# Six DMA transposes of an attention-then-experts kernel moved to TensorE, and their matmuls to earlier slots

## The chip, the cores and the metric

The kernel runs on one core of one Trainium2 chip. The metric is the device time of one execution in microseconds (us).

## The reference, cut to what matters

The first half is attention without softmax: scores are scaled by a decay that depends on the head and on the distance between positions, and masked to be causal. The second half passes every token through four experts and adds their outputs with normalised weights.

```python
# q, k, v: [8 batches, 8 heads, 576 positions, 64]
scores = scale * np.matmul(q, k.transpose(0, 1, 3, 2))
ret = scores * Dmat[None, :, :, :]          # gamma[h] ** (i - j) where i >= j, else 0
attn_out = np.matmul(ret, v)
x = attn_out.transpose(0, 2, 1, 3).reshape(4608, 512)
p = domain_probs / (domain_probs.sum(-1, keepdims=True) + 1e-09)
for e in range(4):                          # w1[e]: 512 x 1024, w2[e]: 1024 x 512
    h = np.maximum(x @ w1[e], 0.0)
    out += p[:, e:e + 1] * (h @ w2[e])
```

## The kernel before

The 4608 tokens are cut into nine tiles of 512. A batch has 576 positions, so tile 0 is batch 0 without its last 64 positions (its "remainder"). Tile 1 needs that remainder and most of batch 1. While TensorE does the expert matmuls of a tile, the attention of the next one is slipped in between them. The expert work of tile 0 is numbered in 32 slots: for each of the four experts four "up" groups (x @ w1, eight 128x512 matmuls, 1.73 us) and four "down" pieces (h @ w2, eight more). After each slot the work registered for it is run:

```python
    for e in range(E):
        for i in range(4):
            up_group(h, 0, e, i)
            run(slots, n)
            n += 1
        for m in range(4):
            down_plain(h, 0, e, m)
            run(slots, n)
            n += 1
```

Batch 1 comes in four "units": unit 0 and 1 are its first 256 positions, for the first and the last four heads, units 2 and 3 the next 256. A unit is cast to bf16 with its decays, k and q are transposed, then follow the scores, the state (`kv`) and the values. In the kernel before, batch 0's units, in the prologue, are transposed on TensorE (`trans_pe`); the remainder and batch 1's units are transposed by DMA from SBUF (the on-chip memory) to SBUF, issued on SyncE's queue:

```python
        # class Unit
        def trans_pe(self, between=0):
            self.qk = atp.tile([128, 2, 2, 2, C], BF16, tag="qkT", name="qkT0")
            pt = ring_tile("pt", [128, 2, 2, 2, 2 * C], BF16)
            for i, n in ((1, "k"), (0, "q")):
                # ... cut
                for r in range(2):
                    for g in range(2):
                        nc.tensor.transpose(pt[:, i, r, g, 0:C], self.bf(n)[:, r, 2 * g:2 * g + 2]..., ident)
            nc.scalar.activation(self.qk..., pt..., Copy)

        def trans_dma(self):
            self.qk = atp.tile([128, 2, 2, 2, C], BF16, tag="qkT", name="qkT1")
            for i, n in ((1, "k"), (0, "q")):
                nc.sync.dma_start_transpose(out=self.qk[:, i]..., in_=self.bf(n)...)
```

The tag `qkT` has two buffers: unit 2 cannot be transposed before unit 0's values have read theirs. The slots, before:

```python
    remainder(slots, 0, (-1, 13, 24, 25))        # cast and transposes, scores, values

    def v_cast(u):
        vs[u].cast("k", nc.vector)
        vs[u].cast("q", nc.vector)
        vs[u].cast("v", nc.scalar)
        vs[u].trans_dma()
        if u == 0:
            load_v(3)

    for u, (c, sc, o) in enumerate(((17, 26, 27), (18, 27, 28), (24, 28, 29), (25, 29, 30))):
        add(c, lambda u=u: v_cast(u))
        add(o, lambda u=u: vs[u].values())
        add(sc, lambda u=u: v_head(u))           # scores and state
    add(26, lambda: [load_p(1, e, nc.sync) for e in range(E)])
    add(27, lambda: load_pair(raw1, 2, 0))       # tile 1's own loads, SyncE's queue too
    add(27, lambda: load_rem(1))
```

Meanwhile the weights (fp32 in HBM, cast to bf16 by the DMA) and batch 1's inputs come in on GpSimd's queue:

```python
    load_w2(2)
    load_v(0)
    load_v(1)
    load_w1(3)
    load_v(2)
    load_w2(3)
```

## Time and profile before

| | before |
|---|---|
| median of 3 runs | 549.27 us (548.95 to 550.24) |
| span of the profiled run | 547.2 us, mean granted TensorE clock 0.997 (1 is full speed) |
| TensorE busy | 529.8 us (97%) |
| tile 0, first up matmul to tile 1's first | 20.11 to 91.33 us: 71.22 us |
| tile 1, the same | 91.33 to 149.81 us: 58.48 us |

The two lines of TensorE's timeline (start, length, what) that bound tile 0:

```profile
20.11 3.12 PE L345 MATMUL ph<-xt,w 128*128 128x512 bf16 x12
91.33 10.52 PE L345 MATMUL ph<-xt,w 128*128 128x512 bf16 x47
```

The page shows the span in 40 slices, each digit a share in tenths (9 is 90% or more):

```profile
PE   8999959999999999999999999999999999999997
PEclk9999989999999999999999999999999999999999
DMA  9999956966446552755177526662555311010001
```

The one dip of TensorE and of its clock between the start and the end is in the sixth slice, 68 to 82 us. The view of waits of TensorE from 48 to 92 us (who waited for whom: us in total, times, longest) names it:

```profile
PE s L526 <- DMA qkT<-bf_q: 5.2, 1, 5.2
PE s L526 <- DMA qkT<-q: 1.1, 1, 1.1
PE ph L345 <- issue: 0.2, 1, 0.2
PE o L589 <- DVE sbd L561: 0.2, 1, 0.2
PE po L364 <- issue: 0.2, 1, 0.2
```

The busy times by stretch, from the end of slot 15 to tile 1:

```profile
core 0: us, PE busy (x) PEld busy (x) DVE busy (x) ACT busy (x) POOL busy (x), PEclk, DMA share, GB/s
48.05:67.60 19.55, 19.45 (x99) 8.78 (x99) 13.79 (x21) 7.98 (x10) 5.40 (x7) 1.00 1.15 226
67.60:72.78 5.18, 0.01 (x3) 0.04 (x2) 1.39 (x2) 0.06 (x1) 0.00 (x0) 1.00 1.26 189
72.78:77.10 4.32, 4.10 (x47) 2.19 (x52) 1.52 (x2) 2.24 (x4) 0.00 (x0) 0.61 0.00 0
77.10:91.33 14.23, 12.46 (x201) 7.10 (x204) 10.06 (x15) 4.90 (x19) 0.00 (x0) 1.00 0.62 153
```

TensorE does nothing for 5.17 us, then works at a granted clock of 0.61 in the mean of 4.32 us (the trace has 0.50 from 72.78 to 76.19 us, then 1.00). The DMA engines are full (1.15 and 1.26: the share is the time of the packets over that of 16 engines, so here packets overlap) until exactly the moment when the gap ends, and then fall idle (0.00). The chain of work that ended last (start, length, what) passes through the same transpose:

```profile
40.15 11.95 DMA rx<-in_q_dram
52.11 20.53 DMA qkT<-bf_q
72.64 0.14 issue
72.78 0.64 PE s L526 x14
73.42 0.85 PE kvp L545 x16
74.27 0.54 PE ph L345
...
78.94 3.03 DMA qkT<-q
81.98 0.14 issue
82.11 0.44 PE s L526 x16
```

Unit 0's q was given to the queue at 52.11 us and landed 20.5 us later; unit 2's, in an emptier queue, took 3.0 us.

### The profile page before, as it was taken

To read this page: it belongs to the slowest core of one execution; us is meant where nothing else is said; L and a number is where in the kernel's file an instruction comes from. 1 tells how busy PE (TensorE), PEld (TensorE's weight loads), DVE (VectorE), ACT (ScalarE), POOL (GpSimd) and SP (SyncE) were. 2 spreads that over 40 slices of the span, in tenths; PEclk is the share of its full clock that TensorE was granted. 3 is DMA by queue.
4 is the path that set the end of the run, shared out by engine and by line. 5 is a ranking of instruction groups with operands and counts; after the bars stand their busy time and mean duration, and the time that the engine had idled before them with its cause. 6 is when DMAs were issued, how large, how long until landed. Compare 5 with 4: busy or idle time off the path is not lost.

```text
span 547.2 us, 10257 instructions
## 1 busy us (share of the span) xinstructions
PE 529.8 (97%) x4255; PEld 340.5 (62%) x4295; DVE 364.6 (67%) x484; ACT 109.2 (20%) x251; POOL 93.1 (17%) x126
## 2 busy tenths in 40 slices
PE   8999959999999999999999999999999999999997
PEld 4544435458844885478646874588448844884486
DVE  5425638986578666886588648865786667557764
ACT  4623331112202230222112211132012200000010
POOL 5734000211112121111112031112021100000000
PEclk9999989999999999999999999999999999999999
DMA  9999956966446552755177526662555311010001
GB/s 240 202 211 248 215 77 174 209 129 139 113 89 142 125 131 67 158 123 146 55 136 170 139 63 115 140 155 78 110 133 107 83 59 38 24 56 19 1 26 52
DMA packets 148126, 64.27 MB, mean 117 GB/s; under 512 B 127248, under 2 KB 138896, under 8 KB 148080
## 3 DMA queue, kind: packets, MB, share of 16 engines
q1 hardware_dynamic: 137760, 44.22, 36.4%
q0 software_dynamic: 10176, 19.27, 16.2%
q8 instruction: 33, 0.54, 0.4%
q10 hardware_dynamic: 144, 0.13, 0.1%
q14 instruction: 13, 0.11, 0.1%
HBM read 53.56 MB, written 9.51 MB: 115 GB/s over the span
## 4 chain that ended last, share of the span: by engine, by line
PE 81%; DMA 11%; DVE 2%; SPq 1%; POOL 1%; issue 1%; ACT 0%; DVEq 0%
PE ph L345 40%; PE pd L437 36%; DMA qkT<-bf_q 4%; DMA wx<-in_moe_w_dram 3%; DMA rx<-in_q_dram 2%; SPq L119 1%; DVE h L351 1%; PE kvp L261 1%; PE s L274 1%; DMA raw_3v<-in_v_dram 1%; PE o L291 1%; DMA qkT<-q 1%; PE o L284 1%; PE po L364 0%; DVE sbd L561 0%
## 5 line engine op out<-in xcount | busy, mean ns | idle before, releaser
L345 PE MATMUL ph<-xt,w 128*128 128x512 bf16 x1118 | 253.2, 380 | 3.2 <-DVE h L351 1.2
L345 PEld LDWEIGHTS <-w 128*128 128x128 bf16 x1152 | 111.3, 98 | 130.8 <-issue 3.0
L351 DVE SCALAR_TENSOR_TENSOR h<-ph,pB 128x1024 bf16<-128x1024 f32 x128 | 155.8, 1222 | 51.0 <-PE ph L345 50.5
L437 PEld LDWEIGHTS <-h 128*128 128x128 bf16 x1024 | 99.2, 98 | 14.1
L437 PEld LDWEIGHTS <-s 128*128 128x128 bf16 x768 | 74.7, 98 | 9.1
L437 PE MATMUL pd<-wx,h 128*128 128x256 bf16 x512 | 61.2, 273 | 0.0
L437 PE MATMUL pd<-wx,s 128*128 128x256 bf16 x512 | 61.2, 273 | 0.0
L222 POOL DMA_DIRECT2D pB<-pd x28 | 15.9, 568 | 165.4 <-DVE h L351 133.7
L266 ACT ACTIVATE sbd<-kvp 64x256 bf16<-64x256 f32 x48 | 18.2, 378 | 104.6 <-PE kvp L261 104.3
L472 POOL TENSOR_TENSOR ob<-v,p 128x256 f32<-128x256 f32 x15 | 10.9, 726 | 153.7 <-DVE v L469 92.7
L276 DVE TENSOR_TENSOR sT<-s,tri 128x1024 bf16<-128x1024 f32 x24 | 29.2, 1217 | 2.2 <-PE s L274 2.2
L454 DVE TENSOR_TENSOR u<-pd,p 128x256 f32<-128x256 f32 x16 | 6.8, 425 | 35.7 <-PE pd L437 35.7
L437 PE MATMUL pd<-t2w,s 128*128 128x256 bf16 x256 | 30.6, 273 | 0.0
L437 PE MATMUL pd<-t3w,h 128*128 128x256 bf16 x256 | 30.6, 273 | 0.0
L437 PE MATMUL pd<-t4w,h 128*128 128x256 bf16 x256 | 30.6, 273 | 0.0
L245 POOL TENSOR_TENSOR bf_q<-raw_q,gq 128x512 bf16<-128x512 f32 x24 | 25.6, 1069 | 22.7 <-DMA raw_q<-in_q_dram 22.4
L364 PE MATMUL po<-wx,h 128*128 128x512 bf16 x124 | 28.4, 379 | 0.4 <-issue 0.2
L445 ACT ACTIVATE p<-pd 128x256 f32<-128x256 f32 x16 | 6.1, 384 | 94.8 <-PE pd L437 83.8
L309 POOL TENSOR_TENSOR bfr_q<-rawr_q,gqr 64x512 bf16<-64x512 f32 x7 | 11.7, 1669 | 71.6 <-DMA out_dram<-acc 42.2
L456 DVE TENSOR_TENSOR oa<-pd,u 128x256 f32<-128x256 f32 x16 | 6.8, 425 | 23.7 <-PE pd L437 23.7
L349 ACT ACTIVATE h<-ph 128x1024 bf16<-128x1024 f32 x16 | 16.4, 1022 | 30.4 <-PE ph L345 29.1
L418 DVE TENSOR_TENSOR s<-h,s 128x1024 bf16<-128x1024 bf16 x32 | 22.4, 739 | 0.0
(141 smaller groups left out, 393.8 us busy)
## 6 DMA issues: line engine op xcount, KB each, us to landing
pB<-pd POOLq DMA_DIRECT2D x28, 256.0 KB, 3.9
raw_k<-in_k_dram SPq DMA_DIRECT2D x48, 128.0 KB, 2.7
raw_q<-in_q_dram SPq DMA_DIRECT2D x48, 128.0 KB, 3.0
raw_v<-in_v_dram SPq DMA_DIRECT2D x48, 128.0 KB, 3.7
wx<-in_moe_w_dram POOLq DMA_DIRECT2D x4, 1024.0 KB, 17.3
out_dram<-oa SPq DMA_DIRECT2D x16, 256.0 KB, 2.1
out_dram<-ob SPq DMA_DIRECT2D x15, 256.0 KB, 2.0
w<-in_moe_w_dram POOLq DMA_DIRECT2D x3, 1024.0 KB, 15.6
```

The costliest lines, as they stand in the source:

```text
L222: eng.dma_start(out=pB[t, e], in_=pd[e:e + 1, t * NT:(t + 1) * NT].to_broadcast([128, NT]))
L245: nc.gpsimd.tensor_tensor(self.bf["q"], raw["q"], gq[:, :, 2 * p:2 * p + 2].unsqueeze(3).to_broadcast([128, NC, 2, D]), op=MULT)
L266: nc.scalar.activation(sbd[r, self.p, :, r], kvp[r, :, :], Copy)
L276: nc.vector.tensor_tensor(self.sT[:, :, :, :].rearrange("p j c t -> p (j c) t"), s[:, :, :, :].rearrange("p j c t -> p (j c) t"), tri[:, : ...
L309: q_engine.tensor_tensor(bfr["q"][0:R], rawr["q"][0:R], gqr[0:R].rearrange("p (g j) -> p g j", j=2).unsqueeze(3).to_broadcast([R, NP, 2, D ...
L345: nc.tensor.matmul(ph[:, f, :], lhsT=w1_sb[e][:, dc, fc * 128:(fc + 1) * 128], rhs=x[:, dc, :], start=(dc == 0), stop=(dc == NDC - 1))
L349: nc.scalar.activation(h[:, fk:fk + 2, :], ph, Relu)
L351: nc.vector.scalar_tensor_tensor(h[:, fk:fk + 2, :], ph, 0.0, pB[t, e][:, :].unsqueeze(1).to_broadcast([128, 2, NT]), op0=MAX, op1=MULT)
L364: nc.tensor.matmul(po[:, g, :], lhsT=h[:, e * NFC + fc, ns * 128:(ns + 1) * 128], rhs=wx[e // 2][:, (e % 2) * NFC + fc, :, :].rearrange("p ...
L418: nc.vector.tensor_tensor(self.alloc("s4")[:, l], h[:, r, self.a], self.s2[:, l], op=SUB)
L437: mm = nc.tensor.matmul(dst, lhsT=src[:, kk, tok], rhs=rhs(c), start=(start and c == 0), stop=(c == KH - 1), skip_group_check=True)
L472: nc.gpsimd.tensor_tensor(self.ob[:, HF:Dm], self.v, self.p5, op=ADD)
```

## The change

The intent: take the six transposes that compete with the loads (remainder k and q, unit 0 and 1 k and q) off the DMA queue, and spread the matmuls that depend on them over the slots of the third and fourth expert. Units 2 and 3 stay on the DMA queue. The diff, with small cuts:

```diff
-    ident = epool.tile([128, 128], BF16)
+    ident = const.tile([128, 128], BF16)
@@ class Rem
-        def trans_dma(self):
+        def alloc_trans(self):
             self.kT = atp.tile([128, NP, 128], BF16, tag="kTr", name="kTr", bufs=1)
             self.qT = atp.tile([128, NP, R], BF16, tag="qTr", name="qTr", bufs=1)
+
+        def trans_pe(self):
+            self.alloc_trans()
+            pt = ring_tile("ptr", [128, 2, NP, 128], BF16)
+            for i, n, w in ((0, "k", 128), (1, "q", R)):
+                for p in range(NP):
+                    nc.tensor.transpose(pt[:, i, p, 0:w], bfr[n][0:w, p, :, :].rearrange("p j d -> p (j d)"),
+                                        ident[0:w, 0:w])
+            nc.scalar.activation(self.kT, pt[:, 0], Copy)
+            nc.scalar.activation(self.qT, pt[:, 1, :, 0:R], Copy)
+
+        def trans_dma(self):
+            self.alloc_trans()
@@ def remainder
-        l, c, s, o = at
+        l, c, tr, s, o = at
-        add(c, x.trans_dma)
+        add(tr, x.trans_pe)
@@ slots
-    remainder(slots, 0, (-1, 13, 24, 25))
+    remainder(slots, 0, (-1, 13, 15, 16, 17))
-        vs[u].trans_dma()
+        if u > 1:
+            vs[u].trans_dma()
-    for u, (c, sc, o) in enumerate(((17, 26, 27), (18, 27, 28), (24, 28, 29), (25, 29, 30))):
+    for u, (c, tr, sc, o) in enumerate(((17, 20, 22, 23), (19, 22, 24, 25), (24, 0, 28, 29), (25, 0, 29, 30))):
+        if u < 2:
+            add(tr, lambda u=u: vs[u].trans_pe())
-    for j, ats in enumerate(((18, 18, 19, 19), (20, 20, 21, 21), (28, 28, 29, 29), (30, 30, 40, 41))):
+    for j, ats in enumerate(((18, 18, 19, 20), (20, 21, 23, 23), (28, 28, 29, 29), (30, 30, 40, 41))):
```

The last pair of lines moves sums of expert weights on VectorE by a slot or two.

## The prediction

> **What bounds the kernel now.** TensorE. The page gives it 97% of a 547.2 us span, and from tile 1 on the chain of waits is almost only its matmuls (57.8 us a tile). The exception is the end of tile 0. Busy times by stretch: from 67.6 to 72.8 us TensorE is idle 5.17 of 5.18 us. The view of waits names one wait, 5.2 us, of batch 1's first score matmuls for a DMA transpose of q, issued at 52.1 us and landed 20.5 us later (the chain; the median is 2.5 us), as it shares the DMA engines with weight and input loads (DMA share 1.15 to 1.26, 190 to 226 GB/s). From 72.8 to 77.1 the granted clock is 0.61: the eight 128x512 matmuls there take 2.8 us, not 1.7, scores and kv 0.5 us more than later. [...] Unit 2's queued transposes cost one more wait of 1.1 us at 81 us; other small waits (state copies) about 0.7 us.
>
> **What the change does.** Six of tile 0's ten DMA transposes (remainder, units 0 and 1) become 24 TensorE transposes plus four ScalarE copies. Work moves from slots 24 to 28 to slots 15 to 25.
>
> - Removed: 5.2 us idle, about 1.6 us of slow clock, 1.1 us wait for unit 2 (its buffer comes free earlier, the queue is empty): 7.9 us, all on the critical path.
> - Added on TensorE: in the prologue four 128x128 transposes show 0.39 to 0.40 us with 0.22 us latency each, so about 60 to 85 ns a piece in a stream: 1.5 to 2.0 us for 24.
> - Added on ScalarE: two copies of 1.02 us, two of about 0.4 to 0.6 us; it was busy 8 of 19.6 us here: off the path.
> - Moved: sums of weights on VectorE, which has 14 of 19.6 us in this stretch; I estimate waits of a few tenths. PSUM has four buffers, one held by the down product: three are left for scores, state, transposes and values. New waits 0.3 to 0.8 us in all.
> - Unit 3's inputs landed at 71 to 72.7 us. Without the transposes they should land earlier; its cast now comes at about 70 us, so VectorE may wait 1 us, with slack before unit 3 is needed at about 79 us.
>
> Net 7.9 − 1.8 − 0.5: about 5.6 us, kept to the end, as tile 1 onward is TensorE-bound with the same work. Tile 1 should begin at about 85.5 us instead of 91.3.
>
> **Predicted: 543.5 us**, 8 in 10 between 541.3 and 546.2. Faster by over 2% (below 538.3) 0.04; within 2% 0.94; slower 0.02. All idle time and slow clock of this stretch, 8.9 us, are 1.6%, so 2% is out of reach unless something else moves.
>
> **What the profile would show.** No TensorE gap over 1 us between 48 and 86 us; granted clock 1.00 throughout; no wait for a DMA transpose of q; 24 more matmuls onto the identity, 60 to 90 ns net each; transposes of units 2 and 3 landing in 2.5 to 4 us; unit 3's inputs landing before 71 us; tile 1's first up matmul at 84.5 to 86.5 us; later tiles unchanged at 57.8 us.
>
> **What would make it wrong.** A new wait in TensorE's order: transposes standing before ready matmuls while the cast or a PSUM buffer is late; VectorE held by unit 3's late inputs, delaying the output accumulation and so a PSUM buffer; the second-half w2 weights late, which the old gap hid; tile 1's own loads (mixing weights, remainder, first pair) late because TensorE now arrives 6 us sooner. Any could give back 1 to 4 us.

## The result, and the profile after

| | before | after |
|---|---|---|
| median | 549.64 us (4 runs, 548.95 to 550.24) | 542.55 us (4 runs, 542.08 to 542.85) |
| ratio, 95% interval | | 0.9871 (0.9854 to 0.9888) |
| span of the profiled run | 547.2 us | 540.9 us |
| tile 0 | 71.22 us | 64.78 us (20.64 to 85.42) |
| tile 1 | 58.48 us | 58.05 us (85.42 to 143.47) |

The lines that bound tile 0 in the kernel after:

```profile
20.64 2.69 PE L358 MATMUL ph<-xt,w 128*128 128x512 bf16 x10
85.42 7.93 PE L358 MATMUL ph<-xt,w 128*128 128x512 bf16 x36
```

A ratio is the mean time of one kernel's fast runs over that of the other's of the same rounds, so not quite the ratio of the medians quoted. The time fell by 7.1 us by the medians and by 6.3 us between the two profiled spans; the runs of before scatter by more than a microsecond, so the sharper measure is the length of tile 0, read from the trace: 6.44 us less. With the 0.43 us of tile 1, and 0.53 us by which the first up matmul came later in this profile, the span is accounted for (−6.44 − 0.43 + 0.53 = −6.34). That start lies between 20.1 and 20.9 us in all profiles, so I take its shift for run-to-run scatter, not for an effect of the change.

The scatter of before goes with the clock. Besides the profiled run, 29 runs of the kernel before have mean granted clock 0.989 to 0.997, 27 of them at 0.995 or below, and the lower the clock, the longer the run (eight at 0.994 took 549.4 us in the mean, nine at 0.991 or below 550.5 us). The profiled run, at 0.997, is at the mild end, so the slow clock probably cost most runs more than the profile shows; no trace of such a run was kept. The four runs of after have 0.999 to 1.000.

The slices of after:

```profile
PE   8999999999999999999999999999999999999997
PEclk9999999999999999999999999999999999999999
DMA  9999947765265635655277517653654211110001
```

Both dips of the sixth slice are gone. TensorE's waits from 48 to 92 us are down to one line:

```profile
PE o L602 <- DVE sbd L574: 0.2, 1, 0.2
```

By stretch:

```profile
core 0: us, PE busy (x) PEld busy (x) DVE busy (x) ACT busy (x) POOL busy (x), PEclk, DMA share, GB/s
48.58:66.20 17.62, 17.62 (x153) 9.00 (x152) 11.65 (x19) 9.23 (x14) 5.39 (x7) 1.00 1.08 253
66.20:72.00 5.80, 5.80 (x71) 2.84 (x69) 5.60 (x10) 4.40 (x9) 0.00 (x0) 1.00 0.04 12
72.00:77.00 5.00, 5.00 (x50) 2.37 (x50) 0.56 (x2) 2.75 (x4) 0.00 (x0) 1.00 0.50 101
77.00:85.42 8.42, 8.04 (x103) 4.26 (x101) 8.21 (x13) 1.87 (x12) 0.00 (x0) 1.00 0.91 232
```

TensorE is idle 0.38 us of 36.84 (before 7.27 of 43.28), the clock is full, and the loads are through about 5 us earlier: the last of them, unit 3's v, landed at 67.9 us instead of 72.7, and unit 3's k 13.7 us after its issue, not 18.4. The chain of waits of this stretch is now TensorE's own work. What it shows of the transposes:

```profile
48.79 0.44 PE ptr L323 x8
49.23 1.83 PE ph L358 x8
51.07 0.12 PE sr L337 x4
...
58.32 0.45 PE pt L516 x8
58.77 3.45 PE po L377 x16
62.22 0.35 PE s L539 x16
62.57 0.60 PE kvp L558 x16
63.17 0.55 PE pt L516 x8
```

The three groups of eight transposes (`ptr`, `pt`, `pt`) take 0.44 + 0.45 + 0.55 = 1.44 us of the chain.

The packets of the two DMA queues in four microseconds (name: packets, MB, share of 16 engines' time), before, from 56 to 60 us; q0 has GpSimd's loads, q1 SyncE's transposes:

```profile
q0 software_dynamic: 430, 1.03, 95.4%
q1 hardware_dynamic: 431, 0.10, 16.6%
```

The queues went one packet for one packet: 362 to 361 from 52 to 56 us, 575 to 573 from 60 to 64, 435 to 436 from 64 to 68. A packet of the loads had about 2.4 KB here, one of the transposes about 240 bytes, so the transposes got a tenth of the bytes. Over the whole run the kernel after sent 3,008 packets less on q1 (134,752, not 137,760), for six transposes. From 60 to 64 us the loads had the engines alone:

```profile
q0 software_dynamic: 765, 0.92, 121.0%
```

This is 765 load packets in four microseconds where the kernel before sent 575.

### The profile page after: what moved, and what is told of

The parts are those of the page before. It is cut to its first block, busy times and chain, and to the rows that moved or that the text cites. A ratio compares the mean times of both kernels' runs of the same rounds, so it can differ in the third digit from the quotient of the medians.

```text
span 540.9 us, 10332 instructions
## 1 busy us (share of the span) xinstructions
PE 532.8 (98%) x4319; PEld 341.3 (63%) x4319; DVE 365.4 (68%) x484; ACT 112.1 (21%) x255; POOL 91.8 (17%) x126
## 3 DMA queue, kind: packets, MB, share of 16 engines
q1 hardware_dynamic: 134752, 43.50, 35.7%
## 4 chain that ended last, share of the span: by engine, by line
PE 92%; DVE 4%; ACT 1%; DMA 1%; issue 0%; SPq 0%; DVEq 0%; ACTq 0%
PE ph L358 44%; PE pd L450 37%; PE po L377 4%; DVE h L364 2%; PE kvp L261 1%; PE s L274 1%; PE o L291 1%; ACT qkT L518 1%; DMA raw_0q<-in_q_dram 1%; PE pt L516 1%; PE o L284 1%; PE s L539 1%; DMA qkT<-bf_q 0%; DVE sT L541 0%; PE kvp L558 0%
## 5 line engine op out<-in xcount | busy, mean ns | idle before, releaser
L241 DVE TENSOR_TENSOR bf_k<-raw_k,gk 128x512 bf16<-128x512 f32 x24 | 21.9, 912 | 0.0
L249 ACT ACTIVATE bf_v<-raw_v 128x512 bf16<-128x512 f32 x24 | 15.1, 628 | 29.8 <-DMA raw_v<-in_v_dram 29.8
```

The source lines that it names most:

```text
L241: nc.vector.tensor_tensor(self.bf["k"], raw["k"], gk[:, :, 2 * p:2 * p + 2].unsqueeze(3).to_broadcast([128, NC, 2, D]), op=MULT)
L249: nc.scalar.activation(self.bf[n], raw[n], Copy)
```

## The experiments

The theory to test: the DMA transposes landed late because they were queued against the loads; TensorE waited, its clock fell, and the change removes that. Three rivals or additions: the order of the slots does it; the transposes are slow by themselves; some of the six moved transposes need not have moved. "Tile 0" below is always the time from its first up matmul to tile 1's first; tile 1 likewise.

### a_pe_old_slots: TensorE transposes, matmuls at the old slots

```diff
-    remainder(slots, 0, (-1, 13, 15, 16, 17))
+    remainder(slots, 0, (-1, 13, 15, 24, 25))
-    ... enumerate(((17, 20, 22, 23), (19, 22, 24, 25), (24, 0, 28, 29), (25, 0, 29, 30))):
+    ... enumerate(((17, 20, 26, 27), (18, 22, 27, 28), (24, 0, 28, 29), (25, 0, 29, 30))):
(the sums of weights at their old slots too)
```

> The kernel after, but the matmuls of the remainder and of units 0 and 1 go back to their old slots (24/25, 26/27, 27/28); only the transposes are on TensorE. Theory 1 (the gain is the DMA transpose taken off the path; the spreading adds nothing by itself): no gap over 0.5 us before the first scores, clock 1.00, time within 1 us of the kernel after, 541.8 to 543.8 us. Rival (the gain needs the matmuls spread over the third and fourth experts, as heads and values close together wait for VectorE and PSUM): at least 2 us of the 7 are lost, 544.5 us or more.

Measured: 544.19 us, ratio 0.9903 (0.988 to 0.9926); tile 0 65.98 us, clock 1.00. TensorE's waits from 20 to 112 us:

```profile
PE s L539 <- DMA qkT<-q: 1.1, 1, 1.1
PE ph L358 <- DVE h L364: 0.4, 1, 0.4
PE o L602 <- DVE sbd L574: 0.2, 1, 0.2
```

It fell between the two expectations: 5.24 of the 6.44 us of tile 0 come from the transposes alone. The other 1.2 us are the wait that the kernel before had too, for unit 2's q: unit 2's transposes were issued only at 72.9 us, after unit 0's values had freed the buffer. VectorE and PSUM (the memory that TensorE writes to), the rival's reason, show no wait of that size.

### b_dma_new_slots: the new slots, all transposes by DMA

```diff
-        add(tr, x.trans_pe)
+        add(tr, x.trans_dma)
-        if u > 1:
-            vs[u].trans_dma()
+        vs[u].trans_dma()
-        if u < 2:
-            add(tr, lambda u=u: vs[u].trans_pe())
```

> The slots of the kernel after, with all transposes by DMA. Theory 1: the transposes still land late (11 us for the remainder, till about 70 to 73 us for the units), TensorE now comes earlier and waits longer: 548 to 556 us, idle of 7 us or more in the stretch from 48 to 75 us, clock below 1. Rival (the order alone gives the gain): 543 us as the kernel after.

Measured: 554.27 us, ratio 1.0091 (1.0064 to 1.0119); tile 0 75.91 us. The wait moved to the remainder's scores, which now come first:

```profile
PE sr L337 <- DMA qTr<-bfr_q: 11.1, 1, 11.1
```

The early slots alone are a loss of 4.7 us in tile 0. The clock was 0.63 in the 3.7 us after this gap. While TensorE stood still the loads went through, and the units' transposes landed 4.2 us after their issue (median of each pair), with no wait for them. The order of the slots is only of use once the transposes are early.

### d_gap_filled: the gap filled with idle matmuls

```diff
 (the kernel before)
+    def fill(n):
+        w = ring_tile("fill", [128, 512])
+        for _ in range(n):
+            nc.tensor.matmul(w, lhsT=w1_sb[0][:, 0, 0:128], rhs=xt_of(0)[:, 0, :], start=True, stop=True)
+
+    add(26, lambda: fill(24))
```

> The kernel before with 24 idle 128x512 matmuls (24 x 0.216 = 5.2 us) put just ahead of batch 1's first scores, to keep TensorE busy while it waits. If about 1.6 us of the stall is the slowed clock after the gap: granted clock 1.00 from 72 to 77 us, first scores at the same 72.8 us, time 1.2 to 1.8 us below the kernel before (about 547.9 us). If the slow clock cost nothing: same time as before, 549.6 us.

Measured: 548.63 us, ratio 0.9986 (0.9966 to 1.0006), which doesn't settle it by the time. The trace does: the first scores start at the same moment (72.72 us) and the stretch after it runs at full clock, to be held against 0.61 before:

```profile
67.45:72.72 5.27, 5.22 (x24) 2.25 (x23) 1.38 (x2) 0.42 (x1) 0.00 (x0) 1.00 1.18 186
72.72:77.23 4.51, 4.30 (x91) 2.72 (x91) 2.00 (x3) 3.23 (x7) 0.00 (x0) 1.00 0.02 4
```

Tile 0 took 70.07 us, 1.15 us less than before. So the slow clock cost about 1.2 us of tile 0 in the profiled run, not the 1.6 that I had worked out. Over the whole span only 0.4 us of it is left (546.8 us, not 547.2); tile 1 took 0.24 us longer. Three of the six runs had a mean clock of 0.996 or 0.997 and are the three longest (548.77 to 549.59 us); they have no trace. In the kernel before, 3.41 us at a clock of 0.50 followed the 5.17 us of idleness; with the gap filled the clock stayed at 1.00: the slow clock belongs to the gap.

### f_before_no_w2_3 and f2_before_no_w13_w23: the loads taken away

Both are the kernel before with weights of the last expert set to zero instead of loaded, so the result is wrong.

```diff
 (f_before_no_w2_3)
-    load_w2(3)
+    nc.gpsimd.memset(wx[1][:, NFC:2 * NFC, :, :], 0.0)
 (f2_before_no_w13_w23, in addition)
-    load_w1(3)
+    nc.gpsimd.memset(w1_sb[3], 0.0)
```

> The kernel before with the load of the last expert's second weights (1 MB written, 2 MB read, in the queue from 51.6 us) replaced by zeros; the result is wrong on purpose, TensorE's work is the same. Theory A (unit 0's q transpose lands at 72.6 us because it shares the DMA engines with the weight and input loads, which end at the same time): the DMA engines fall idle at 62 to 65 us, the transpose lands there, no wait above 0.3 us at batch 1's first scores, clock 1.00, time 6 to 8 us below the kernel before. Theory B (the six queued DMA transposes are slow by themselves): it lands at about 72 us still and the time is within 2 us of the kernel before.

Measured: 543.59 us, ratio 0.989 (0.9863 to 0.9918); tile 0 65.86 us, clock 1.00. Unit 0's q landed at 68.96 us, 3.7 us earlier than before, and TensorE still waited 1.2 us for it. Neither theory was met: A had it at 62 to 65 us, B at 72. (The zeros took GpSimd 3.5 us and so sent unit 3's loads about 1.7 us later, which blurs the run a little.) Less load helps, but by less than its own share; the count of packets, made after this run, gave a better form of A: the transposes get every second packet as long as any load is queued (431 of 861 from 56 to 60 us in the kernel before). This is not the whole account: counted in the order of issue, the last packet of unit 0's q was through at 69.0 us in the kernel before, yet the transpose landed at 72.6 us. The records don't tell the 16 engines apart, so that rest stays open. The next run tested the new form.

> The run without the last expert's second weights, with its first weights (2 MB read, in the queue from 43.8 us) replaced by zeros as well; wrong on purpose. In the kernel before, the transposes' packets and the loads' packets went one for one from 52 to 68 us (361 to 362, 431 to 430, 573 to 575, 436 to 435 by 4 us), and six transposes are about 3,000 packets. If the transposes wait because they get only every second packet while loads are queued: with both loads gone, unit 0's q lands by 60 us, no wait at batch 1's first scores, clock 1.00, unit 2's wait of 1.1 us stays; tile 0 takes 64.5 to 65.5 us (71.2 before, first up matmul of tile 0 to that of tile 1), time about 543 us. If the six transposes are slow by themselves, unit 0's q still lands after 66 us and tile 0 takes 66 us or more.

Measured: 543.47 us, ratio 0.9879 (0.986 to 0.9898); tile 0 64.76 us, clock 1.00 in the profiled run (0.996 or 0.997 in the other three, without a trace). Unit 0's q landed 8.7 us after its issue at 52.02 us, so at 60.7 us, and nothing waited for it at 67.8 us; unit 2's wait stayed (1.4 us). From 56 to 60 us:

```profile
q0 software_dynamic: 133, 0.42, 45.0%
q1 hardware_dynamic: 1208, 0.28, 44.9%
```

The transposes sent 1,208 packets where they had sent 431 in the kernel before. The same six transposes with a thinner load queue land in time: they are not too slow by themselves. The transposes also cost the loads time: with all loads present, taking the six away let the last load land about 5 us earlier (67.9 us, not 72.7).

### c_rem_dma: the remainder back on the DMA queue

```diff
 (the kernel after)
-        add(tr, x.trans_pe)
+        add(tr, x.trans_dma)
-    remainder(slots, 0, (-1, 13, 15, 16, 17))
+    remainder(slots, 0, (-1, 13, 13, 24, 25))
```

> The kernel after with the remainder's two transposes back on the DMA queue and its matmuls at slots 24 and 25 as before; units 0 and 1 stay on TensorE. If the remainder's eight transposes are pure cost (0.44 us of TensorE in the chain, and nothing waited for the DMA in the kernel before): 0.4 us faster than the kernel after, about 542.1 us, no wait at the remainder's scores. Rival (its DMA transposes hold up the weight and input loads, or the matmuls at slots 24 and 25 crowd unit 1): 543 us or more.

Measured: 541.46 us (five runs, 541.27 to 541.67), ratio 0.9853 (0.9833 to 0.9873); tile 0 64.23 us, 0.55 us less than in the kernel after, and no wait at the remainder's scores. The remainder's transposes are issued at 47 us and needed at 66 us by the old slots, so even a slow landing is early enough, and its eight TensorE transposes are a pure cost (0.44 us of the chain in the kernel after). (The run moves the remainder's matmuls back too; how the 0.55 us divide between the two is not shown.) Tile 1 gave 0.22 us back (58.27 us). This is the lowest time measured. Its interval overlaps that of the kernel after, and the two ran in different calls, so by times alone it isn't proven faster; the trace shows 0.3 us over both tiles.

### e_all_units_pe: units 2 and 3 on TensorE as well

```diff
 (the kernel after)
-    ... (24, 0, 28, 29), (25, 0, 29, 30))):
+    ... (24, 26, 28, 29), (25, 27, 29, 30))):
-        if u > 1:
-            vs[u].trans_dma()
-        if u < 2:
+        if True:
```

> The kernel after, with units 2 and 3 transposed on TensorE too (transposes at slots 26 and 27), so 16 more TensorE transposes and no DMA transpose left in batch 1's units. In the kernel after nothing waits for those four DMA transposes, so if a TensorE transpose is pure cost of 0.055 to 0.06 us where the DMA one is not waited for: about 0.9 us slower than the kernel after, 543.4 us. Rival (DMA transposes cost something wherever they stand, by holding up tile 1's loads): as fast as the kernel after or faster, 542.5 us or less.

Measured: 543.05 us, ratio 0.9882 (0.9866 to 0.9899); tile 0 65.69 us, 0.91 us longer than in the kernel after, for 16 more transposes: 57 ns each, if all of it is theirs. Tile 1 took 57.81 us, 0.24 us less, so the rival has a small part. A TensorE transpose cost its stream time here (these 57 ns), and was worth it only where the DMA one was waited for.

### g_unit1_dma: unit 1 back on the DMA queue

```diff
 (the kernel after)
-    ... (17, 20, 22, 23), (19, 22, 24, 25), ...
+    ... (17, 20, 22, 23), (18, 0, 27, 28), ...
-        if u > 1:
+        if u > 0:
-        if u < 2:
+        if u < 1:
```

> The kernel after with unit 1 back on the DMA queue and at its old slots (cast 18, scores 27, values 28); remainder and unit 0 on TensorE. With four of six transposes gone the loads end near 66 us (as in the kernel after, plus about 2 us), so unit 1's two DMA transposes should land by 68 to 70 us, before its scores at about 73 us: no wait there; 0.5 us of TensorE saved; but unit 3 gets its transpose buffer only after unit 1's values, so a wait of up to 1 us as unit 2 had in the run with the old slots may come back: 541.8 to 543.5 us. If unit 1's transposes are starved as unit 0's were: a wait of 2 us or more at slot 27 and 545 us or more.

Measured: 542.89 us, ratio 0.9879 (0.986 to 0.9899); tile 0 64.33 us (0.45 less), with a wait of 0.4 us at unit 3's scores, as foreseen; tile 1 58.10 us. Unit 1's q took 12.6 us and was in time. A gain in tile 0 that the time does not show.

### h_only_unit0_pe, h3_only_unit0_pe_3buf and a3_old_slots_3buf: both together, and a buffer more

`h` joins the edits of `c` and `g`. The other two give one unit's transposed pair a buffer of its own (borrowed from the mixing weights' pool), `h3` unit 1's in `h`, and `a3` unit 0's in `a_pe_old_slots`:

```diff
-            self.qk = atp.tile([128, 2, 2, 2, C], BF16, tag="qkT", name="qkT1")
+            own = (self.b, self.hf, self.g) == (1, 0, 1)          # a3: (1, 0, 0), in trans_pe
+            self.qk = (ppool if own else atp).tile([128, 2, 2, 2, C], BF16, tag="pB" if own else "qkT", name="qkT1")
```

> Only unit 0 on TensorE: remainder by DMA at slots 13, 24, 25 and unit 1 by DMA with scores at slot 27, values at 28. The two single changes took tile 0 from 64.8 us to 64.2 (remainder by DMA) and 64.3 (unit 1 by DMA). If they add up: tile 0 at 63.8 us, time about 541.3 us, waits of 0.4 to 1 us at unit 3's scores. If four DMA transposes in the loads' way starve again: a wait of 1 us or more at unit 1's scores, and tile 0 at 65 us or more.

Measured: 544.89 us (six runs, 544.32 to 547.91), ratio 0.9916 (0.9893 to 0.994); tile 0 65.04 us, tile 1 59.54 us. The savings did not add up: with four transposes in the queue unit 1's q took 18.0 us and TensorE waited 0.8 us for it, and tile 1 waited 1.0 us for the transposes of its remainder.

> As the run with only unit 0 on TensorE, with unit 1's transposed pair in a buffer of its own, so that unit 3's DMA transposes need not wait for unit 1's values. The wait of 0.4 us at unit 3's scores goes: tile 0 at 63.3 to 63.6 us, time about 541.0 us. Rival (that wait hid another, of VectorE or of the loads): tile 0 as without the buffer.

Measured: 543.12 us, ratio 0.9874 (0.9855 to 0.9893); tile 0 64.51 us, tile 1 58.03 us. Unit 3's wait went, and so did those of tile 1; tile 0 missed the expected 63.3 to 63.6 us, because unit 1's q was still waited for (0.2 us) and a down piece waited 0.4 us for ScalarE. No better than `c_rem_dma`.

> The run with TensorE transposes at the old slots, with unit 0's transposed pair in a buffer of its own, so that unit 2's DMA transposes need not wait for unit 0's values. If the 1.1 us that this order lost to the kernel after is that one buffer: no wait at unit 2's scores, tile 0 takes 64.8 us (66.0 with two buffers, 64.8 in the kernel after), time 542.6 us. If it is the crowding of heads and values on VectorE and PSUM: the wait goes and others of 0.5 us or more come in its place, tile 0 at 65.5 us or more.

Measured: 543.86 us, ratio 0.9896 (0.9876 to 0.9917). Tile 0 took 64.82 us: the 1.2 us that the old slots lost there were that one buffer, as supposed. But the time did not follow; tile 1 took 60.57 us. The profiled run was the longest of the four (545.52 us, the others 543.63 to 543.88), so in the others tile 1 probably lost less than the 2.5 us seen here. TensorE's waits from 48 to 110 us:

```profile
PE sr L337 <- DMA qTr<-bfr_q: 1.3, 1, 1.3
PE s L274 <- DMA qkT<-bf_q: 1.0, 1, 1.0
PE s L540 <- DMA qkT<-q: 0.5, 1, 0.5
```

The first two are tile 1's own transposes, the third is unit 3's. SyncE issued its DMAs in the order of the program: unit 3's transposes, issued at 76.4 us when unit 1's buffer came free, stood ahead of tile 1's loads, and the last of these were issued at 90.2 us, 4.8 us into tile 1; in the kernel after unit 3's are issued at 73.4 us and tile 1's last load at 85.7 us, 0.3 us into tile 1. The slots of the kernel after pay twice: by the buffer, and by the queue that is clear in time for the next tile. Why `a_pe_old_slots` and `g_unit1_dma`, whose queues were nearly as late (last loads at 89.0 and 88.5 us), show no such wait is only a matter of margin as far as I can see: they came out 1 to 2 us earlier.

## Why the prediction was right

It gave 543.5 us, 541.3 to 546.2, and "within 2%"; the median was 542.55 us. Point by point, with the terms of its sum held against tile 0's 6.44 us:

| term | predicted | measured |
|---|---|---|
| idle before batch 1's first scores | 5.2 us | 5.17 us, gone |
| slow clock after it | 1.6 us | about 1.2 us (d_gap_filled, one trace) |
| wait for unit 2's q | 1.1 us | 1.14 us, gone |
| other idle time of the stretch | 0, taken as staying | 0.6 us less (7.27 − 5.17 − 1.14 = 0.96, now 0.38) |
| 24 transposes on TensorE | −1.5 to −2.0 us | −1.44 us |
| new waits | −0.3 to −0.8 us | none |
| sum | 5.6 us | 5.17 + 1.2 + 1.14 + 0.6 − 1.44 = 6.7 us, 6.44 by the trace |

- The cause was right and is shown: the gap and the slow clock belong to the one late transpose (d), the transposes on TensorE alone bring most of the gain (a), the slots alone lose (b), and without most of the loads the DMA transposes land in time (f2).
- "Shares the DMA engines with weight and input loads" was right but coarse. It is packet for packet, one to one (431 to 430 from 56 to 60 us), with packets of a tenth of the size (about 240 bytes, not 2.4 KB); f, which was expected to follow the bytes, showed that the coarse form gives wrong numbers.
- The gain of tile 0 was put about 0.8 us too small (5.6, not 6.44 us). The mis-sized terms are the new waits in PSUM and on VectorE, put at 0.5 us, which did not come, and the small waits that also went; the transposes cost 57 to 60 ns each and not 60 to 85. The slow clock was over-sized by 0.4 us: I had added up the lengths of matmul records, which overlap (the first scores' run to 73.42 us, the state's begin at 73.17); from the first scores to the first values the stretch took 4.22 us before and 2.99 us in d_gap_filled. It errs the other way than the rest, so the sum came out closer than its terms: in part luck.
- "Unit 2's wait goes as its buffer comes free earlier" was right, and a3 shows that it is the buffer.
- The checks named in advance: no gap over 1 us, right; clock 1.00, right; tile 1 at 84.5 to 86.5 us, right (85.42); unit 3's inputs before 71 us, right (its k at about 66.3 us, its v at 67.9); transposes of units 2 and 3 in 2.5 to 4 us, at the edge (2.4 to 2.5). "Later tiles unchanged at 57.8 us" was right in that nothing was given back: tile 1 was 0.43 us shorter.
- Missed by the prediction altogether: that the remainder's transposes did not need to move. Its old slots were late enough; moving it costs 0.55 us of tile 0.

## What to carry to other kernels

The DMA transposes here sent many small packets (about 240 bytes) and, beside bulk loads, got one packet for each of theirs (431 to 430): plan for the landing under load (11 to 20 us here), not for the landing alone (2.4 us), or transpose on TensorE, at some 57 ns for 128x128 here, where the result is waited for and only there. An order that looks like a matter of matmuls also sets when buffers and an in-order DMA queue come free (unit 3's transposes were issued at 76.4 us in `a3_old_slots_3buf`, at 73.4 in the kernel after): look for the lost microsecond in the next stage, as the run with the additional buffer had to. When times scatter by a microsecond, measure a stage between two fixed instructions of the trace.

## What else the runs show, and what they leave open

- Alone, the DMA transposes landed in 2.4 us (units 2 and 3 in the kernel after), much like the k loads of 128 KB on the same queue (2.7 us in the median, kernel before). Beside bulk loads they landed in 11.5 to 20.5 us, with about 240 bytes to a packet against about 2.4 KB, and the last load landed about 5 us earlier without the six of them (67.9 us, not 72.7).
- The counts of packets (431 to 430) do not explain that the remainder's transposes, issued at 46.9 and 48.3 us, moved only 23 packets from 48 to 52 us, while the loads moved 371: the first came at 51.5 us, 4.6 us after the issue (1.3 us in the kernel after for unit 2, with no load queued). No run here settled this.
- One record of a 128x128 transpose on TensorE is 219 ns long, but nearly all of it overlaps in a stream: 16 more transposes added 0.91 us in `e_all_units_pe`, 57 ns each, if all of it is theirs.
- After 5.2 us idle the granted clock was 0.50 for 3.41 us, and 1.00 with the gap filled (`d_gap_filled`). For the cost, the slow time multiplied by the share of the clock withheld gives an estimate of 3.41 x 0.5 = 1.7 us; here it was about 1.2 us.
